# Second MoE: seven-product up products on halves of 256 columns, one plain block of 256 tokens, TensorE's order written out

## The chip, the cores and the metric

The kernel runs on one core of one Trainium2 chip. The metric is the device time of one execution in microseconds (us); three executions of the kernel before have a median of 1143.99 us (1142.7 to 1144.92).

## The reference

Three steps follow one another. An attention with a memory term (4 batches, 8 heads, 576 positions, 64 wide) gives 2304 tokens of 512 values. The first MoE is a gated layer of width 1536, the second a layer of width 2048 with a bounded square:

```python
g = x @ w_gate                      # 2304x512 @ 512x1536
silu = g * (1.0 / (1.0 + np.exp(-g)))
x = silu * (x @ w_val) @ w_out      # first MoE: back to 2304x512
h = x @ w_in                        # second MoE: 2304x512 @ 512x2048
g = np.where(h >= 1, h, np.where(h <= -1, 0.0, (h + 1) ** 2 / 4.0))
out = g @ w_out                     # 2304x512
```

Weights arrive as float64 words. Each product is made to about fp32 exactness out of two fp32r parts (hi and lo) of both operands, so that one tile product costs three matmuls: hi by lo, lo by hi, hi by hi (`PARTS`).

## The kernel before, in words

A program of tasks (`Plan`) is built in Python. Each task has an engine, a cost, a priority, the tasks it depends on and the buffer places that it uses. `Plan.order` simulates the engines with these costs and emits the instructions in the order of the simulation, so every engine's order is fixed at build time; at run time the engines wait for each other by semaphores. All large DMAs are issued by SyncE (SP) in the same order, and an SP instruction that waits holds up those behind it.

**Attention** (up to about 345 us) also makes gate and value products of the first six width units for tokens 0 to 1535 and stores them to DRAM (`early_unit`, `gv`). **The first MoE** then runs over six blocks of 384 tokens (`BLOCK`): first the remaining early products (all eight early units for the two late blocks, units 6 and 7 for the others), then block by block twelve width units. `hidden` makes one: either it loads gate and value from `gv`, or TensorE makes them (`up_matmuls`, moving operand 384 columns); ScalarE and VectorE form the product and split it into hi and lo (`ends_of`); `down` adds its share into four PSUM banks (moving operand `h`, 384 columns). At the end of a block `pieces` copies the four banks out and stores seven pieces of the block (`ys`).

**The second MoE** uses a seven-product scheme (Winograd's form of Strassen's). For a pair of width units and a block the up product is a 2x2 by 2x2 product of blocks: 256 by 128 blocks of weights, and halves of the block of tokens (`HB`, 192 columns). Seven block products of six matmuls each (42 in all) take the place of eight (48). Sums of weight blocks are made when a pair is decoded (`Weights.pair`: three places of 512 KB and one of 256 KB), sums of tokens in `pieces`. `hidden2` (L1343) issues the products: t1 and t5 into two banks, t6, t2, t7, t4 accumulate into them. In between ScalarE copies a bank (`seed`, `keep`) before TensorE goes on accumulating in it, and VectorE adds two results (v1, v2); t4 waits for v2. Each of the two results goes through relu, square, bound, hi and lo, and `down` (L1416) multiplies it by the second weights: per width unit nine matmuls of 512 columns for the three 128-token groups of a block.

The 16 width units form eight pairs, in three phases of 2, 3 and 3 pairs (`PHASES`). Each phase goes over all six blocks, loads the block's seven pieces (`load_y`), and adds into partial sums that are kept in DRAM between phases (`part`). In which order TensorE takes the products and the `down` groups is left to the priorities of the plan.

The weights of the second MoE are decoded from float64 by VectorE and ScalarE in the background. Of the first three pairs (`PARK`) the decoded places are stored to DRAM while the first MoE runs, and fetched back before their use (`parked`, `back`); the other five are decoded into place during the second MoE. SBUF has 25 unit places (`UNITS`), six half places (`HALVES`), 15 places for token pieces (`XB`).

Of the kernel before, what the change touches and what calls it, by code (L numbers as in the profile page):

```python
# [18 lines left out]
P = 128  # L19
# [21 lines left out]
XB, OP, RAW, HP, TP, WA = 15, 5, 3, 3, 3, 5  # L41
SU = 2
UNITS, HALVES = 25, 6
PHASES = (2, 3, 3)
PARK = 3
# [4 lines left out]
BLOCK = 384  # L50
# [210 lines left out]
def e_pe(n, cols):  # L261

    return n * (cols + (32 if cols >= 320 else 18)) / 2.4
# [879 lines left out]
def tile_attention_two_moe(  # L1143
# [14 lines left out]
    NB = NT // BLOCK  # L1158
    ys = [[dram.tile([P, 4 * HB], F32, name=f"ys{b}_{k}") for k in range(7)] for b in range(NB)]
    part = [[dram.tile([P, DM], F32, name=f"part{b}_{m}") for m in range(BLOCK // P)] for b in range(NB)]  # L1160
# [96 lines left out]
    plan.cap("W", UNITS, range(UNITS1))  # L1257
    for tag, n in (("wh", HALVES), ("xb", XB), ("hp", HP), ("tp", TP), ("op", OP), ("su", SU), ("mm", 4), ("acc", 4),
                   ("gv", 3), ("dd", 1)):
        plan.cap(tag, n)  # L1260
# [6 lines left out]
    blocks = [slice(e, e + BLOCK) for e in range(0, NT, BLOCK)]  # L1267
# [15 lines left out]
    def ends_of(s, t, src, uses):  # L1283


        def hi():
            s["h"] = hp.tile([P, 2, BLOCK], F32R, name="h", tag=f"h{s['i'].slot}")
            nc.scalar.copy(s["h"][:, 0], s["t"])  # L1288

        def lo():  # L1290
            nc.vector.tensor_sub(s["h"][:, 1], s["t"], f32(s["h"][:, 0]))  # L1291

        t = plan.add("ACT", e_act(BLOCK), s["at"], hi, [t], [s["it"], s["i"]])
        s["done"] = plan.add("DVE", e_dve2(BLOCK), s["at"], lo, [t], [s["it"], s["i"]])
        return s

    def start_of(base):
        return {"i": plan.inst("hp"), "it": plan.inst("tp"), "at": base}

    def mk_t(s):  # L1300
        s["t"] = tp.tile([P, BLOCK], F32, name="t", tag=f"t{s['it'].slot}")
        return s["t"]

    def hidden(f, tok, base, x, kind):


        s = start_of(base)
        if kind == 0:
            i_g, i_v = plan.inst("xb"), plan.inst("gv")

            def load():
                s["gv"] = xb.tile([P, 2, BLOCK], F32, name="gv", tag=f"xb{i_g.slot}")
                nc.sync.dma_start(s["gv"], gv[f][:, :, tok])

            src = [(lambda j=j: s["gv"][:, j], i_g) for j in range(2)]
            t_g = plan.dma(base - 25, [BLOCK * 2.85], load, uses=[i_g, i_v], behind=xlast.get(plan))
            xlast[plan] = plan.last
        else:
# [3 lines left out]
            def prod():  # L1322
                for j, u in enumerate(units):
                    s[j] = mm.tile([P, HT], F32, name="mm", tag=f"mm{banks[j].slot}")
                    up_matmuls(nc, s[j][:, 0:BLOCK], u, x["x"], slice(0, BLOCK))

            t_g = plan.add("PE", e_pe(len(units) * 12, BLOCK), base + 1, prod,
# [3 lines left out]
            src = [(lambda j=j: s[j][:, 0:BLOCK], i_p) for j, i_p in enumerate(banks)]  # L1331
# [7 lines left out]
        t = plan.add("ACT", e_act(BLOCK) + 60, base, silu, [t_g] + (downs[-2:-1] if kind else downs[-3:-2]), [src[0][1], s["it"]])  # L1339
        t = plan.add("DVE", e_dve2(BLOCK), base, product, [t, t_g], [src[1][1], s["it"]] + ([i_v] if kind == 0 else []))  # L1340
        return ends_of(s, t, src, [])

    def hidden2(pair, y, base, up):  # L1343


        banks = i_a, i_e = [plan.inst("mm") for _ in range(2)]
        i_d, i_k, i_s, i_u = plan.inst("acc"), plan.inst("dd"), plan.inst("su"), plan.inst("su")
        s = {}
        two = [start_of(base), start_of(base)]
        lf, rt = slice(0, HB), slice(HB, BLOCK)  # L1350

        def product(k, out, first):
            for j in range(2):
                for i, (pw, px) in enumerate(PARTS):
                    nc.tensor.matmul(out, pair["k"](k, pw, j), y["x"][k][:, px, j], start=first and not (i or j),  # L1355
                                     stop=(j == 1 and i == 2), skip_group_check=True)

        def some(*todo):
            for k, name, first in todo:
                if name not in s:  # L1360
                    i = i_d if name == "d" else (i_a, i_e)[name == "e"]
                    s[name] = (acc if name == "d" else mm).tile(
                        [P, HT], F32, name=("acc" if name == "d" else "mm"), tag=f"{i.tag}{i.slot}")
                product(k, s[name][:, lf], first)

        def pe(prio, todo, deps, uses, **kw):
            ks = [k for k, *_ in todo]
            return plan.add("PE", e_pe(6 * len(todo), HB), prio, lambda: some(*todo),
                            deps + [y["t"][k] for k in ks], uses + pair["i"] + [y["i"][k] for k in ks], **kw)

        def keep(name, src):
            def f():
                i = i_s if name == "s5" else i_u
                s[name] = su.tile([P, HB], F32, name=name, tag=f"su{i.slot}")
                nc.scalar.copy(s[name], s[src][:, lf])  # L1375
            return f

        def seed():
            s["e"] = mm.tile([P, HT], F32, name="mm", tag=f"mm{i_e.slot}")
            nc.scalar.copy(s["e"][:, lf], s["a"][:, lf])  # L1380

        cost = e_act(HB)
        t1 = pe(up + 1, [(0, "a", True)], pair["t"], [i_a, i_e], behind=(ups or [None])[-1])
        ups.append(t1)
        t5 = pe(up, [(4, "d", True)], [t1], [i_d, i_k])
        c1 = plan.add("ACT", cost, base - 10, seed, [t1], [i_a, i_e])
        c5 = plan.add("ACT", cost, base - 10, keep("s5", "d"), [t5], [i_d, i_s])
        t6 = pe(up - 10, [(5, "a", False)], [t5, c1], [i_a])
        c2 = plan.add("ACT", cost, base - 10, keep("u2", "a"), [t6], [i_a, i_u])
        t2 = pe(up - 10, [(1, "e", False), (2, "d", False)], [t6, c5], [i_e, i_d])  # L1390
        t7 = pe(up - 10, [(6, "a", False)], [t2, c2], [i_a])
        v1 = plan.add("DVE", e_dve2(HB), base - 10,
                      lambda: nc.vector.tensor_add(s["e"][:, rt], s["u2"], s["d"][:, lf]), [c2, t2], [i_e, i_d, i_k, i_u])  # L1393
        v2 = plan.add("DVE", e_dve2(HB), base - 10,
                      lambda: nc.vector.tensor_add(s["a"][:, rt], s["s5"], s["a"][:, lf]), [t7, c5], [i_a, i_s])
        t4 = pe(up - 10, [(3, "a", False)], [v2], [i_a])
        for h, (name, i_p, t) in enumerate((("e", i_e, v1), ("a", i_a, t4))):
            o = two[h]
            src = lambda name=name: s[name][:, 0:BLOCK]

            def relu(o=o, src=src):
                nc.scalar.activation(mk_t(o), src(), AF.Relu, bias=half, scale=0.5)  # L1402

            def square(o=o):
                nc.scalar.activation(o["t"], o["t"], AF.Square)  # L1405

            def bound(o=o, src=src):
                nc.vector.scalar_tensor_tensor(o["t"], src(), 1.0, o["t"], op0=ALU.max, op1=ALU.min)  # L1408

            t = plan.add("ACT", e_act(BLOCK), base, relu, [t], [i_p, o["it"]])  # L1410
            t = plan.add("ACT", e_act(BLOCK), base, square, [t], [o["it"]])
            t = plan.add("DVE", e_dve2(BLOCK), base, bound, [t], [i_p, o["it"]])
            ends_of(o, t, None, [])
        return two
# [22 lines left out]
    def pieces(state, b, base, t_d, later):  # L1437
# [5 lines left out]
        places = [plan.inst("xb") for _ in range(7)]  # L1443
        st = {}
        lf, rt = slice(0, HB), slice(HB, BLOCK)
# [8 lines left out]
        def copies(eng, m0, left, right):  # L1454
            def f():
                for cols, k in ((lf, left), (rt, right)):
                    for j in range(2):
                        eng(raw(k)[:, j], state[m0 + j][:, cols])
            return f

        ca = plan.add("ACT", 4 * e_act(HB), base, copies(nc.scalar.copy, 0, 0, 6), [t_d],
                      [*state["i"][:2], places[0], places[6]])
        cb = plan.add("DVE", 4 * e_dve2(HB), base, copies(nc.vector.tensor_copy, 2, 1, 2), [t_d],
                      [*state["i"][2:], places[1], places[2]])
        sub = nc.vector.tensor_sub
        d1 = plan.add("DVE", e_dve2(BLOCK), later, lambda: sub(raw(4), raw(6), raw(0)), [ca],
                      [places[0], places[4], places[6]])
        d2 = plan.add("DVE", e_dve2(BLOCK), later, lambda: sub(raw(5), raw(2), raw(4)), [cb, d1],
                      [places[2], places[4], places[5]])
        d3 = plan.add("DVE", e_dve2(BLOCK), later, lambda: sub(raw(6), raw(2), raw(6)), [d1, cb],  # L1470
                      [places[2], places[6]])
        d4 = plan.add("DVE", e_dve2(BLOCK), later, lambda: sub(raw(3), raw(1), raw(5)), [d2],
# [134 lines left out]
```

## Time and profile before

| | |
|---|---|
| median of three executions | 1143.99 us |
| profiled execution, its own time | 1142.59 us |
| span of that execution on the core | 1140.8 us |
| TensorE matmul busy | 1109.7 us, 97% |
| TensorE weight load busy (beside the matmuls) | 1013.6 us, 89% |
| VectorE, ScalarE, GpSimd busy | 769.1, 677.5, 257.8 us |
| granted TensorE clock, mean over the span | 0.994 of full speed |

Matmuls are pipelined, so a record lasts longer than the distance to the next one. What a matmul costs TensorE in a stream is the distance from start to start: the start of the next row less the start of this one, over the count. The three stages stand in the trace at 0 to 345.5 us (attention), 345.5 to 703 us (first MoE) and 703 us to the end (second MoE).

### The profile page before, as it was taken

The page shows a single profiled execution, that of the slowest core. Times are in us where ns is not written, and L with a number is a line of the kernel's source. Part 1 is how long each engine was busy: PE and PEld are TensorE (multiplying, and loading weights), DVE is VectorE, ACT ScalarE, POOL GpSimd, SP SyncE. Part 2 cuts the span into 40 slices and gives each one's busy share as a digit, 9 for nine tenths or more (in the row PEclk, how much of TensorE's full clock was granted, in tenths as well). Part 3 has the DMA queues.
Part 4 walks back from the last instruction along what each step waited for, and adds up shares of the span by engine and source line. Part 5 has one row for each costly group of instructions (what it writes and reads, how often), then busy time and mean ns, then how long its engine had stood idle before and what let it go on. Part 6 is the DMA issues. An engine that isn't in the chain of part 4 may idle for free.

```text
span 1140.8 us, 20230 instructions
## 1 busy us (share of the span) xinstructions
PE 1109.7 (97%) x6864; PEld 1013.6 (89%) x6864; DVE 769.1 (67%) x1863; ACT 677.5 (59%) x1650; POOL 257.8 (23%) x325
## 2 busy tenths in 40 slices
PE   6998999999999999999999999999999999999998
PEld 4566887898889999999999999899999999999997
DVE  5689979988872888888962553876677335734334
ACT  6888989999882355454542433755655444544443
POOL 6898779666560000000000000000000000000000
PEclk9999999999999999999999999999999999999999
DMA  5566556756538889769796639986755456545412
GB/s 137 161 181 173 138 148 165 198 145 162 168 98 301 294 278 384 226 245 354 271 338 202 238 132 383 389 294 216 254 194 185 162 180 219 175 157 183 150 57 83
DMA packets 181816, 240.04 MB, mean 210 GB/s; under 512 B 73936, under 2 KB 127184, under 8 KB 181712
## 3 DMA queue, kind: packets, MB, share of 16 engines
q1 hardware_dynamic: 181136, 237.69, 63.9%
q8 instruction: 55, 0.90, 0.3%
q10 hardware_dynamic: 576, 1.05, 0.2%
q14 instruction: 49, 0.40, 0.1%
HBM read 163.98 MB, written 67.63 MB: 203 GB/s over the span
## 4 chain that ended last, share of the span: by engine, by line
PE 78%; ACT 8%; DMA 6%; DVE 2%; issue 2%; POOL 1%; SPq 0%; POOLq 0%; ACTq 0%; DVEq 0%
PE acc L1426 30%; PE mm L1138 20%; PE mm L1355 14%; PE acc L1355 6%; PE av L868 3%; DMA KK<-KK 2%; ACT a L682 2%; PE s L669 1%; DMA raw<-in_moe_w_gate_dram 1%; DMA raw<-in_moe_w_out_dram 1%; ACT R L398 1%; PE t L807 1%; DMA gv<-gvo 1%; ACT KK L398 1%; PE s L703 1%
## 5 line engine op out<-in xcount | busy, mean ns | idle before, releaser
L1426 PE MATMUL acc<-wu,h 128*128 128x512 f32 x864 | 215.0, 394 | 1.6 <-DVE h L1291 1.6
L1138 PE MATMUL mm<-xb,wu 128*128 128x384 f32 x1152 | 204.2, 334 | 0.9 <-ACT gvo L1186 0.9
L1138 PEld LDWEIGHTS mm<-xb,wu 128*128 128x128 f32 x1152 | 200.1, 188 | 1.3 <-ACT gvo L1186 1.2
L1426 PEld LDWEIGHTS acc<-wu,h 128*128 128x128 f32 x864 | 156.0, 189 | 31.5 <-DVE h L1291 2.2
L1288 ACT CAST h<-t 128x384 fp32r<-128x384 f32 x168 | 85.7, 513 | 130.4 <-PE acc L1426 69.9
L1426 PE MATMUL acc<-h,wu 128*128 128x384 f32 x864 | 154.2, 334 | 0.3 <-DVE h L1291 0.3
L1426 PEld LDWEIGHTS acc<-h,wu 128*128 128x128 f32 x864 | 150.0, 188 | 0.7 <-DVE h L1291 0.7
L1355 PE MATMUL mm<-xb,wu 128*128 128x192 f32 x1152 | 149.0, 273 | 0.0
L1355 PEld LDWEIGHTS mm<-xb,wu 128*128 128x128 f32 x1152 | 143.8, 191 | 4.8
L1291 DVE TENSOR_TENSOR h<-t,h 128x384 fp32r<-128x384 f32 x168 | 92.2, 556 | 68.2 <-ACT h L1288 67.7
L1138 PE MATMUL mm<-xh,wu 128*128 128x512 f32 x432 | 115.7, 406 | 0.9 <-DMA xh<-xs 0.6
L1402 ACT ACTIVATE t<-mm,half 128x384 f32<-128x384 f32 x96 | 55.2, 581 | 93.3 <-DVE mm L1393 51.1
L760 POOL TENSOR_SCALAR a<-a,r,OGP 128x256 f32<-128x256 f32 (+3 forms) x144 | 96.1, 677 | 29.3 <-DVE r L751 10.9
L1408 DVE SCALAR_TENSOR_TENSOR t<-mm,t 128x384 f32<-128x384 f32 x96 | 52.9, 555 | 65.0 <-ACT t L1405 64.9
L1138 PEld LDWEIGHTS mm<-xh,wu 128*128 128x128 f32 x432 | 78.0, 191 | 16.0 <-DMA xh<-xs 1.5
L1355 PE MATMUL acc<-xb,wu 128*128 128x192 f32 x576 | 79.9, 274 | 0.3 <-ACT s L1375 0.2
L682 ACT ACTIVATE a<-a,mn 128x128 f32<-128x128 f32 (+3 forms) x128 | 71.1, 559 | 10.5 <-DVE mn L675 10.0
L1355 PEld LDWEIGHTS acc<-xb,wu 128*128 128x128 f32 x576 | 72.5, 192 | 1.2 <-ACT s L1375 0.4
L955 ACT ACTIVATE wA<-raw 128x512 f32<-128x512 f32 x64 | 43.1, 673 | 46.4 <-DMA raw<-in_moe_w_out_dram 23.1
L1186 ACT COPY gvo<-mm 128x384 f32<-128x384 f32 (+1 forms) x84 | 43.4, 524 | 36.6 <-PE mm L1138 23.0
L1393 DVE TENSOR_TENSOR mm<-u,acc 128x192 f32<-128x192 f32 x48 | 17.3, 361 | 68.4 <-PE acc L1355 68.1
L675 DVE CUSTOM_DVE_ANT_0 a<-s,mask 128x256 f32<-128x256 f32 (+3 forms) x128 | 57.7, 484 | 5.9 <-PE s L669 3.6
(158 smaller groups left out, 1842.1 us busy)
## 6 DMA issues: line engine op xcount, KB each, us to landing
xb<-ys SPq DMA_DIRECT2D x126, 384.0 KB, 4.2
xb<-xs SPq DMA_DIRECT2D x48, 384.0 KB, 6.4
gv<-gv SPq DMA_DIRECT2D x48, 384.0 KB, 5.1
ys<-yo SPq DMA_DIRECT2D x42, 384.0 KB, 3.9
raw<-in_moe_w_out_dram SPq DMA_DIRECT2D x28, 512.0 KB, 4.7
xs<-x SPq DMA_DIRECT2D x16, 576.0 KB, 3.3
gv<-gvo SPq DMA_DIRECT2D x48, 192.0 KB, 4.4
part<-oo SPq DMA_DIRECT2D x36, 256.0 KB, 2.2
```

Of the source, the lines that this page charges most:

```text
L675: nc.vector.tensor_tensor_reduce(a, st[f"s{h}{c}"][:, 0:kl], self.mask0[:, 512 - kl:512], -0.125, 3.0e38, ALU.add, ALU.min, mn[:, o:o + 1])
L682: nc.scalar.activation(a, a, AF.Exp, bias=mn[:, o:o + 1], scale=-1.0, accum_out=sm[:, o, 0:1])
L760: nc.gpsimd.tensor_scalar(a, a, st["mn"]["r"][:, o:o + 1], self.OGP[:, n, o:o + 1], op0=ALU.mult, op1=ALU.mult)
L955: nc.scalar.activation(f32(s["F"]), f32(words(s["raw"])[:, :, 1]), AF.Abs)
L1138: nc.tensor.matmul(out, kt_of(unit, pw, kt), x[kt][:, px, cols], start=(kt == 0 and i == 0), stop=(kt == KT - 1 and i == 2))
L1186: nc.scalar.copy(s["o", j], s[j][:, 0:gt])
L1288: nc.scalar.copy(s["h"][:, 0], s["t"])
L1291: nc.vector.tensor_sub(s["h"][:, 1], s["t"], f32(s["h"][:, 0]))
L1355: nc.tensor.matmul(out, pair["k"](k, pw, j), y["x"][k][:, px, j], start=first and not (i or j), stop=(j == 1 and i == 2), skip_group_check ...
L1402: nc.scalar.activation(mk_t(o), src(), AF.Relu, bias=half, scale=0.5)
L1408: nc.vector.scalar_tensor_tensor(o["t"], src(), 1.0, o["t"], op0=ALU.max, op1=ALU.min)
L1426: nc.tensor.matmul(state[m][:, 0:n], l, r, start=(begin and i == 0), stop=(end and i == 2), skip_group_check=True)
```

## The change

- `BLOCKS` replaces the six equal blocks: four of 512 tokens and one of 256 (tokens 1536 to 1791), which is the second in order. Both stages use it. `HB` becomes 256.
- In the second MoE the blocks of 512 keep the seven-product form, now with 256 columns (`hidden2`). The block of 256 tokens takes the plain eight products (`hidden1`), which read three stored pieces instead of seven.
- TensorE's instructions of the second MoE are one chain (`next_pe`, each behind the last). `down2` does half of a `down` (two 128-token groups, six matmuls); the halves of the pair before stand in `queue`, and `fill` puts one after t5, one before t4 and the rest after t4. The third bank of `hidden2` comes from the pool `mm`, since a block of 512 tokens takes all four banks of `acc`.
- In phases 1 and 2 the plain block comes last (`ORDERS`). The last block of the first MoE takes the units that need products first (`LAST`).
- All eight pairs are parked. They are decoded into three unit places and one half place of their own (tags `B`, `Bh`), and `fetch_pair` brings them back: for the coming phase from the third block of a phase on.
- Places: `XB` 15 to 12 (each a third larger), `UNITS` 25 to 20, `HALVES` 6 to 5.

The diff, cut to its core:

```diff
-XB, OP, RAW, HP, TP, WA = 15, 5, 3, 3, 3, 5
+XB, OP, RAW, HP, TP, WA = 12, 5, 3, 3, 3, 5
-UNITS, HALVES = 25, 6
+UNITS, HALVES = 20, 5
-PARK = 3
-BLOCK = 384
+BLOCK = 512
+BLOCKS = ((0, 512), (1536, 256), (512, 512), (1024, 512), (1792, 512))
+LAST = (8, 9, 10, 11, 0, 1, 2, 3, 4, 5, 6, 7)
+ORDERS = ((0, 1, 2, 3, 4), (0, 2, 3, 4, 1), (0, 2, 3, 4, 1))
 HB = BLOCK // 2
...
-    return n * (cols + (32 if cols >= 320 else 18)) / 2.4
+    return n * (cols + (32 if cols >= 320 else 25)) / 2.4
...
+    plan.cap("B", 3 + UNITS, range(UNITS))
+    plan.cap("Bh", 1 + HALVES, range(HALVES))
...
+    def next_pe(cost, prio, fn, deps, uses):
+        seq.append(plan.add("PE", cost, prio, fn, deps, uses, behind=seq[-1:]))
+        return seq[-1]
+
+    def fill(n):
+        for go in queue[:n]:
+            go()
+        del queue[:n]
+
+    def hidden1(pair, y, base, ahead):
+        two = []
+        for todo in (((0, 0), (1, 1)), ((4, 0), (3, 2))):
+            i_p, s = plan.inst("mm"), start_of(base, HB)
...
+            t = next_pe(e_pe(12, HB), base, prod, pair["t"] + [y["t"][piece] for _, piece in todo],
+                        [i_p] + pair["i"] + [y["i"][piece] for _, piece in todo])
+            if not ahead:
+                fill((len(queue) + 1) // 2 if not two else len(queue))
+            two.append(bounded(s, t, i_p, lambda s=s: s["p"][:, 0:HB]))
+        return two
...
+        t1 = pe([(0, "a", True)], pair["t"], [i_a, i_n])
+        t5 = pe([(4, "d", True)], [], [i_d, i_k])
+        c1 = add_act(lambda: nc.scalar.copy(bank("e")[:, lf], s["a"][:, lf]), [t5], [i_a, i_e])
+        c5 = add_act(keep("s5", "d", i_s), [t5], [i_d, i_s])
+        fill(1)
+        t6 = pe([(5, "a", False)], [c1], [i_a])
+        c2 = add_act(keep("u2", "a", i_u), [t6], [i_a, i_u])
+        t2 = pe([(1, "e", False), (2, "d", False)], [c5], [i_e, i_d])
+        t7 = pe([(6, "a", False)], [c2], [i_a])
+        v1 = add_dve("e", "u2", "d", [c2, t2], [i_e, i_d, i_k, i_u])
+        v2 = add_dve("a", "s5", "a", [t7, c5], [i_a, i_s])
+        fill(1)
+        t4 = pe([(3, "a", False)], [v2], [i_a, i_n])
+        fill(len(queue))
...
-            pairs[p] = wts.pair(plan, "W", "wh", [in_cols(moe2_w_in, f) for f in (2 * p, 2 * p + 1)], pr, behind, p < PARK)
+            pairs[p] = wts.pair(plan, "B", "Bh", [in_cols(moe2_w_in, f) for f in (2 * p, 2 * p + 1)], pr, behind, True)
...
+    def fetch_pair(ph, i, after):
+        p, pr = first_of[ph] + i, at_(ph, 0) + 20 * i - 15
+        for s in (pairs[p], w_out[2 * p], w_out[2 * p + 1]):
+            wts.back(plan, s, ("W", "W", "W", "wh"), pr, fetched + after)
+            fetched[:] = [s["load"]]
...
     for ph, count in enumerate(PHASES):
+        last = ph == len(PHASES) - 1
+        for k, b in enumerate(ORDERS[ph]):
+            tok, at0 = blocks[b], at_(ph, k)
+            y = load_y(b, at0, [t_last] if ph == 0 else [], y["last"], free=0) if ph or k else y0
+            if not last and 1 < k:
+                fetch_pair(ph + 1, k - 2, [y["last"]])
...
+                hid = hidden2 if size(tok) == BLOCK else hidden1
+                for j, s in enumerate(hid(pairs[p], y, pb, last and k == len(blocks) - 1 and i == count - 1)):
+                    for ms in ((0, 1), (2, 3))[:state["n"] // 2]:
+                        queue.append(lambda s=s, state=state, ms=ms, base=pb, p=p, f=2 * i + j, b=b, at0=at0, count=count,
+                                     last=last: down2(s, state, ms, base + 25, w_out[2 * p + f % 2], f == 0,
+                                                      f == 2 * count - 1, last, b, at0))
+    fill(len(queue))
```

## Rows read from the trace of the kernel before

**Rows 1.** The page: busy time, share of the span and instructions by engine.

```profile
PE 1109.7 (97%) x6864; PEld 1013.6 (89%) x6864; DVE 769.1 (67%) x1863; ACT 677.5 (59%) x1650; POOL 257.8 (23%) x325
```

**Rows 2.** Busy time by stage: from:to, us, engines (instructions), clock, DMA share, GB/s.

```profile
345.50:703.20 357.70, 356.46 (x2038) 353.44 (x2037) 239.62 (x497) 153.27 (x324) 1.43 (x1) 1.00 0.80 277
703.20:1140.80 437.60, 431.76 (x2917) 394.14 (x2916) 246.73 (x516) 224.28 (x506) 0.00 (x0) 1.00 0.58 198
```

**Rows 3.** TensorE's waits from 345 us on: who for whom, us, times, longest.

```profile
PE acc L1426 <- DVE h L1291: 2.0, 3, 0.9
PE mm L1138 <- ACT gvo L1186: 0.9, 1, 0.9
PE acc L1355 <- ACT s L1375: 0.2, 1, 0.2
```

**Rows 4.** Timeline of TensorE in the second MoE: start, length, instruction, tiles, shape, count.

```profile
905.66 0.81 PE L1355 MATMUL mm<-xb,wu 128*128 128x192 f32 x6
906.31 0.83 PE L1355 MATMUL acc<-xb,wu 128*128 128x192 f32 x6
906.98 2.24 PE L1426 MATMUL acc<-wu,h 128*128 128x512 f32 x9
909.05 1.48 PE L1355 MATMUL mm<-xb,wu 128*128 128x192 f32 x12
...
911.74 0.64 PE L1426 MATMUL acc<-wu,h 128*128 128x512 f32 x2
```

**Rows 5.** Timeline of TensorE's weight loads in the same stretch.

```profile
910.98 0.75 PEld L1355 LDWEIGHTS acc<-xb,wu 128*128 128x128 f32 x6
911.65 0.19 PEld L1426 LDWEIGHTS acc<-wu,h 128*128 128x128 f32 x1
```

**Rows 6.** Timeline of TensorE in the attention, two matmuls of 256 columns, then 128.

```profile
261.76 0.28 PE L669 MATMUL s<-KK,SX 128*128 128x256 f32 x1
...
262.00 0.33 PE L669 MATMUL s<-KK,SX 128*128 128x128 f32 x2
```

**Rows 7.** The chain of waits in the first MoE, a stretch of 384-column matmuls.

```profile
474.55 4.16 PE acc L1426 x24
```

**Rows 8.** Timeline of TensorE, a stream of 512 columns and the next start.

```profile
345.51 12.79 PE L1138 MATMUL mm<-xh,wu 128*128 128x512 f32 x54
358.13 0.34 PE L1138 MATMUL mm<-xb,wu 128*128 128x384 f32 x1
```

**Rows 9.** Timeline of TensorE at the seam of the two MoEs.

```profile
703.18 0.81 PE L1355 MATMUL mm<-xb,wu 128*128 128x192 f32 x6
703.83 6.43 PE L1426 MATMUL acc<-h,wu 128*128 128x384 f32 x36
...
719.42 2.34 PE L1426 MATMUL acc<-wu,h 128*128 128x512 f32 x9 [0.78 <-DVE h L1291]
```

**Rows 10.** Groups of ScalarE and VectorE in the second MoE: busy, mean ns, idle before.

```profile
L1402 ACT ACTIVATE t<-mm,half 128x384 f32<-128x384 f32 x96 | 55.2, 581 | 93.3 <-DVE mm L1393 51.1 <-PE mm L1355 42.1
...
L1375 ACT COPY u<-mm 128x192 f32<-128x192 f32 x48 | 15.3, 319 | 21.9 <-PE mm L1355 18.2 <-DVE mm L1395 1.9 <-DVE h L1291 0.7
...
L1018 DVE TENSOR_TENSOR wu<-wA,wu 128x512 fp32r<-128x512 f32 x15 | 10.3, 687 | 2.1 <-ACT wu L1016 2.1
```

**Rows 11.** SP's queue: the first raw weights of the second MoE, and all parks.

```profile
467.18 0.99 SPq L950 DMA_DIRECT2D raw<-in_moe_w_in_dram  x2
...
L1023 SPq DMA_DIRECT2D park<-wu x15: 319/332/923, 481.6 to 578.0; - x15
```

**Rows 12.** DMA issues: piece loads (count, KB, us to landing), and the longest in the chain.

```profile
xb<-ys SPq DMA_DIRECT2D x126, 384.0 KB, 4.2
...
808.37 10.20 DMA raw<-in_moe_w_out_dram
```

**Rows 13.** Timeline at the end of the kernel.

```profile
1134.60 2.34 PE L1426 MATMUL acc<-wu,h 128*128 128x512 f32 x9 [0.87 <-DVE h L1291]
1135.60 2.07 DVE L1564 TENSOR_TENSOR oo<-oo,acc 128x512 f32<-128x512 f32 x3 [1.05 <-PE acc L1426]
```

## What I predict, and why

> **What bounds the kernel now.** I read the page first: TensorE's matmuls are busy 97% of the span [rows 1]. A busy share of pipelined matmuls says little by itself, so I read next what TensorE waits for. From 345 us to the end it waits for other engines 3.1 us in all [rows 3], in some 790 us: both MoEs are bound by TensorE's own stream. Last I read what a matmul costs there, from start to start in the timelines:
> - 192 columns: 12 in 906.98 - 905.66 = 1.32 us, then 24 in 911.74 - 909.05 = 2.69 us [rows 4]; together 36 in 4.01 us, **111.4 ns** each.
> - 384 columns: 24 in 4.16 us [rows 7], **173.3 ns**.
> - 512 columns: 9 in 909.05 - 906.98 = 2.07 us [rows 4], **230 ns**; in a long stream 54 in 358.13 - 345.51 = 12.62 us [rows 8], **233.7 ns**.
> - 256 columns: two in 262.00 - 261.76 = 0.24 us [rows 6], so about **118 to 120 ns**. Such pairs stand only in the attention.
>
> From 384 to 512 columns the price per column holds (0.451 and 0.449 to 0.456 ns), and 256 columns fit (0.46 to 0.47). At 192 it is 0.58: the line through 256 and 384 would give some 91 ns, and 20 ns are lost. The weight loads show where: in a 192-column run one starts every (911.65 - 910.98)/6 = 112 ns [rows 5], the matmuls' own pace. A matmul of 192 columns is over before the next 128x128 weights are in; one of 256 columns lasts longer than the load.
>
> The model closes. The second MoE has 6 blocks x 8 pairs x 42 = 2016 matmuls of 192 columns (224.6 us) and 6 x 3 x 16 x 3 = 864 of 512 (199.6 us at 231). With 36 matmuls of the first MoE that run in its stretch [rows 9] (6.2 us) that is 430.4 us; from 703.18 us [rows 9] to the last matmul's end, 1134.60 + 2.34 = 1136.94 us [rows 13], it is 433.8. Of the 3.4 us left, 0.8 and 0.9 are two waits [rows 9, 13].
>
> **The change, part by part**, against the profiled execution (1142.59 us), which is 1.4 us under the median of the three runs.
>
> *Up products of the second MoE.* Four blocks of 512 need 4 x 8 x 42 = 1344 matmuls of 256 columns, the plain block 8 x 2 units x 4 x 3 = 192: 1536 in all. At 118.5 ns that is 182.0 us instead of 224.6: **-42.6 us**. Columns hardly change (393216 for 387072); 480 matmuls at the weight load's pace go. The row [rows 6] stands between other shapes, so both ends: not under the loads' pace, 111.4 ns (171.1 us, -53.5), and not likely over 124 ns, the line's price with 5 ns of jitter (190.5 us, -34.1). The `down` matmuls stay at 864 of 512 columns.
>
> The Trainium skill (TensorE: Matmul & The Clock Gate, "LDWEIGHTS (loading the stationary operand)") gives a weight load its columns over 1.2 GHz, 107 ns for 128; the loads' 112 ns [rows 5] lie 5 ns above that and bear the rule out. The same page ("Back-to-back issue gap") puts an isolated matmul at N/2.4 + 2.5 ns, 109 ns for 256 columns, under this trace's 118 to 120; by it, as an estimate, the up products would take some 168 us. The measured pair decides here.
>
> *First MoE.* 6 x 12 x 12 = 864 `down` matmuls of 384 columns become 576 of 512 and 144 of 256; 1152 products become 720 of 512 and 288 of 256. Before: 2016 x 173.4 = 349.6 us. After: 1296 of 512 at 231.5 (between 230 and 233.7) and 432 of 256 at 118.5: 300.0 + 51.2 = 351.2 us, **+1.6** (-4 if 512 columns cost 227, +5 at 234). 288 matmuls fewer bring nothing, because 512 columns cost as much per column as 384.
>
> *Start of the first MoE.* The one wait there, 0.9 us for ScalarE's copies [rows 3], comes from stores of gate and value. Five buffers of 256 columns hold two thirds of what five of 384 did, while 256-column products run first: **+1** (0 to 4).
>
> *Seam of the MoEs.* With 12 piece places, `y0` holds seven and five are left for the seven pieces of the last block, so VectorE's sums must wait until two have been stored; the next block's pieces wait for these sums. The first pair has no older `down` to put between its products, so t6 waits for ScalarE's copy and t4 for VectorE's sum. Before, the seam cost 0.78 us at 719 us [rows 9] and little else. **+3** (0 to 10).
>
> *TensorE's written order.* Each pair of 512 tokens has four guarded steps. t1 or t5 is 6 x 118.5 = 0.71 us, half a `down` 6 x 231 = 1.39 us. Behind t5, t6 waits for c1, with 1.39 us of `down` as cover; a 192-column copy takes 0.32 us [rows 10], so one of 256 some 0.4 us. t7 waits for c2 under t2 (1.42 us), t4 for v2 under the second half `down` (1.39 us). All fit with over 0.5 us to spare, as long as ScalarE and VectorE are free; an operation of 0.6 to 0.7 us in front [rows 10] eats that. What is queued behind such a wait is all of TensorE. The chain to the first `down` of a result is relu, square, bound, hi, lo: five steps of 0.6 to 0.7 us (0.58 us at 384 columns, 0.69 us on VectorE at 512 [rows 10]) and the handovers, about 4.8 us, against 6.9 us of TensorE's work between. The copies' wait before was 0.2 us in all 48 pairs [rows 3]. For 40 pairs **+2** (0 to 8).
>
> *Weights.* Five more pairs are stored and fetched: some 28 MB more traffic (twice five pairs of 5 x 512 + 256 KB), with no new work on the compute engines. Three pairs passed the decoder from 467 to 578 us [rows 11], 37 us each; eight at that pace end at 467 + 296 = 763 us. The last is needed in phase 2, from about 703 + 96 + 144 = 943 us on. TensorE hides it with 180 us to spare, and the DMA queues, at 0.80 and 0.58 of their time in the two stages [rows 2], have room. Nothing on the path; were the pace 60 us a pair, it would start to show.
>
> *Tail.* The last block has two 128-token groups instead of three: one VectorE sum of 2.07/3 = 0.69 us less [rows 13]; and the last pair's own `down` stands behind 2.8 us of older `down`, which covers the wait of 0.87 us [rows 13]. **-1.5.**
>
> Sum: -42.6 + 1.6 + 1 + 3 + 2 - 1.5 = -36.5. 1142.59 - 36.5 = 1106.1, with 1.4 for the median **1107.5 us**.
>
> **Rivals.**
> 1. *256 columns run at the weight load's pace.* If only the load limits, 111.4 ns instead of 118.5: 10.9 us less, **1097 us**. Against it: the pair in rows 6, and that 256 lies on the line of the larger sizes. To this side the Trainium skill's isolated gap leads (TensorE: Matmul & The Clock Gate, "Back-to-back issue gap"). 0.13.
> 2. *The seam and the written order cost more.* One strict chain gives up what the plan did before, to take whatever is ready. 0.5 us lost in each of 40 pairs, or one late pieces' load per block visit of some 1.5 us: 15 to 20 us, **1125 us**. For it: ScalarE and VectorE still decode weights in the first phases. Against it: the covers above. 0.17.
> 3. *Slower: pieces arrive late at every block visit.* The place is `load_y` on SP's queue. Of 12 places the running block holds seven, so the next block's last two pieces are asked for only when t1 and t5 of the running block's last pair are done. From there to t7 of the next block are 9.1 + 4.9 = 14 us. A piece took 4.2 us at 384 KB [rows 12], some 5.6 at 512 KB; the longest load on the chain took 10.2 us [rows 12]. Eleven visits would each have to lose 3.7 us to eat the gain, that is loads of 18 us: **1148 us**. SP would have to be held up behind a fetch or a store for that. 0.05.
> 4. *DMA of parked weights holds back the first MoE as well*, a milder form: **1135 us**. 0.03.
>
> **How the numbers follow.** My forecast, 1101 to 1113 us, has 0.62; the rivals have 0.13, 0.17, 0.05 and 0.03. The range takes rival 1 to about 1096 (256 columns at 111) and rival 2 to 1124: 1096 to 1124 holds some 0.8. A measurement of this kernel can tell about 0.2% (2.3 us) from no change; all cases but rival 3 lie far below: faster 0.94, same 0.01, slower 0.05.
>
> **What would show it.** Right: in the second MoE six 256-column matmuls start to start in 0.71 us, weight loads no longer at their own pace; 512 columns at 230 ns in the first MoE; TensorE's waits from 345 us on under 12 us; the second MoE some 390 us long. Wrong: a pitch of 112 or over 124 ns; waits on ScalarE's copies or on `h` that recur per pair; waits on piece loads at the block visits; first MoE products beyond 234 ns; VectorE still decoding after 800 us with TensorE waiting for weights.

## The result and the profile after

The changed kernel takes **1113.85 us** (median of four, 1111.40 to 1115.46) against 1143.35 us beside it: a ratio of 0.9739, 95% interval 0.9714 to 0.9764, so 2.6% faster. The forecast was 1107.5 us with a range of 1096 to 1124. The sign and the main term came out as forecast. The time lies 6 us above the forecast: waits, and what the clock took behind them, cost more than was booked.

The page's engine line of the changed kernel; its span is 1113.4 us:

```profile
PE 1069.7 (96%) x6096; PEld 921.0 (83%) x6096; DVE 767.4 (69%) x1754; ACT 656.8 (59%) x1506; POOL 256.8 (23%) x325
```

Against [rows 1], TensorE has 768 instructions fewer, and the weight loads' share falls from 89% to 83%. The timeline of TensorE in the second MoE, changed kernel (start, length, instruction, shape, count), answers to [rows 4]:

```profile
860.73 3.04 PE L1373 MATMUL mm<-xb,wu 128*128 128x256 f32 x24
863.61 1.55 PE L1625 MATMUL acc<-wu,h 128*128 128x512 f32 x6
864.99 0.88 PE L1373 MATMUL mm<-xb,wh 128*128 128x256 f32 x6
865.71 2.91 PE L1625 MATMUL acc<-wu,h 128*128 128x512 f32 x12
868.45 1.60 PE L1373 MATMUL mm<-xb,wu 128*128 128x256 f32 x12
```

24 matmuls of 256 columns take 863.61 - 860.73 = 2.88 us, 120.0 ns each, above the 112 ns of a weight load [rows 5], so that the loads no longer set the pace. The written order is there too: t6, t2 and t7 (24 matmuls), half a `down`, t4, two halves, t1 and t5. The chain of waits in the first MoE, answering to [rows 7]:

```profile
612.64 5.44 PE mm L1140 x24
```

24 matmuls of 512 columns in 5.44 us, 226.7 ns each. By stage (from:to, us, engines, clock, DMA share, GB/s), answering to [rows 2], and the 120 us around and behind the seam:

```profile
345.50:699.50 354.00, 346.33 (x1711) 295.73 (x1711) 251.14 (x482) 151.46 (x285) 1.44 (x1) 0.99 0.79 279
699.50:1113.40 413.90, 403.23 (x2473) 361.99 (x2471) 228.46 (x423) 205.25 (x401) 0.00 (x0) 0.99 0.74 277
700.00:820.00 120.00, 114.33 (x676) 101.55 (x675) 71.47 (x134) 64.23 (x126) 0.00 (x0) 0.97 0.99 381
```

The second MoE's DMA share has risen from 0.58 to 0.74, and from 700 to 820 us the queues are full (0.99). TensorE's waits from 345 us on (who for whom, us, times, longest), answering to [rows 3]:

```profile
PE mm L1140 <- ACT gvo L1188: 5.2, 1, 5.2
PE acc L1625 <- DVE h L1298: 4.0, 3, 2.0
PE mm L1373 <- DVE mm L1439: 3.0, 2, 2.2
PE acc L1469 <- DVE h L1298: 2.4, 1, 2.4
```

They have grown from 3.1 to 14.6 us. And behind each long wait stands something that my sum did not have. Windows of the changed kernel before, just behind and after the wait of 5.2 us, then behind two more (the clock is the figure before the last two):

```profile
364.00:370.00 6.00, 6.00 (x53) 6.00 (x52) 4.78 (x11) 0.68 (x2) 0.00 (x0) 1.00 1.08 380
375.60:381.10 5.50, 5.50 (x25) 5.50 (x26) 3.76 (x9) 1.97 (x5) 0.00 (x0) 0.50 0.50 186
381.20:387.00 5.80, 5.80 (x49) 5.80 (x49) 5.80 (x14) 2.17 (x5) 0.00 (x0) 0.99 0.52 163
725.60:729.30 3.70, 3.70 (x13) 3.16 (x14) 3.45 (x6) 2.12 (x5) 0.00 (x0) 0.56 0.90 296
800.90:804.20 3.30, 3.30 (x11) 2.60 (x10) 2.66 (x6) 2.20 (x4) 0.00 (x0) 0.53 0.91 356
```

TensorE looks fully busy from 375.6 to 381.1 us, but it starts 25 matmuls where 49 to 53 fit into stretches of like length: the granted clock is 0.50, the lower of its two levels (1.2 instead of 2.4 GHz). Behind the wait of 2.4 us it is the same, by the count: 24 matmuls in 4.63 us, where 24 x 0.12 us and the last one's end make 3.0; the granted clock is 0.62 from 548.1 to 552.6 us.

```profile
548.15 4.63 PE L1469 MATMUL acc<-h,wu 128*128 128x256 f32 x24 [2.43 <-DVE h L1298]
```

### The profile page after: what moved, and what is told of

The parts are those of the page before. It is cut to its first block, busy times and chain, and to the rows that moved or that the text cites. A ratio compares the mean times of both kernels' runs of the same rounds, so it can differ in the third digit from the quotient of the medians.

```text
span 1113.4 us, 18370 instructions
## 1 busy us (share of the span) xinstructions
PE 1069.7 (96%) x6096; PEld 921.0 (83%) x6096; DVE 767.4 (69%) x1754; ACT 656.8 (59%) x1506; POOL 256.8 (23%) x325
## 4 chain that ended last, share of the span: by engine, by line
PE 80%; ACT 7%; DMA 5%; DVE 3%; issue 1%; POOL 1%; SPq 0%; ACTq 0%; DVEq 0%; POOLq 0%
PE mm L1140 23%; PE acc L1625 18%; PE mm L1373 16%; PE acc L1469 13%; PE av L870 4%; PE s L671 2%; DMA gv<-gvo 1%; ACT a L684 1%; DMA KK<-KK 1%; PE t L809 1%; PE s L705 1%; ACT KK L400 1%; ACT R L400 1%; DMA gv<-gv 1%; PE s L667 1%
## 5 line engine op out<-in xcount | busy, mean ns | idle before, releaser
L1140 PE MATMUL mm<-xb,wu 128*128 128x512 f32 (+1 forms) x1008 | 203.8, 362 | 5.2 <-ACT gvo L1188 5.2
L1373 PE MATMUL mm<-xb,wu 128*128 128x256 f32 x1296 | 168.6, 283 | 0.0
L1469 PE MATMUL acc<-h,wu 128*128 128x512 f32 (+1 forms) x720 | 153.2, 371 | 2.4 <-DVE h L1298 2.4
L1298 DVE TENSOR_TENSOR h<-t,h 128x512 fp32r<-128x512 f32 (+1 forms) x140 | 88.3, 635 | 57.7 <-ACT h L1295 57.0
L1295 ACT CAST h<-t 128x512 fp32r<-128x512 f32 (+1 forms) x140 | 80.3, 576 | 80.6 <-PE acc L1469 31.4
L1357 ACT ACTIVATE t<-mm,half 128x512 f32<-128x512 f32 (+1 forms) x80 | 51.8, 648 | 93.7 <-PE mm L1373 47.2
L684 ACT ACTIVATE a<-a,mn 128x128 f32<-128x128 f32 (+3 forms) x128 | 71.1, 558 | 12.5 <-DVE mn L677 12.1
L1188 ACT COPY gvo<-mm 128x512 f32<-128x512 f32 (+1 forms) x80 | 43.2, 545 | 57.4 <-PE mm L1140 41.0
L1363 DVE SCALAR_TENSOR_TENSOR t<-mm,t 128x512 f32<-128x512 f32 (+1 forms) x80 | 50.7, 634 | 32.1 <-ACT t L1360 32.1
L1439 DVE TENSOR_TENSOR mm<-u,mm 128x256 f32<-128x256 f32 x32 | 13.7, 429 | 85.6 <-PE mm L1373 81.5
L404 DVE TENSOR_TENSOR R<-t,R 128x384 fp32r<-128x384 f32 (+3 forms) x120 | 53.3, 483 | 4.5 <-ACT R L400 3.8
L968 DVE SCALAR_TENSOR_TENSOR wA<-raw,wA 128x512 uint32<-128x512 uint32 x68 | 55.2, 815 | 0.4
```

The lines of the kernel that those rows point to most:

```text
L404: nc.vector.tensor_sub(lo(), src(), f32(hi()))
L684: nc.scalar.activation(a, a, AF.Exp, bias=mn[:, o:o + 1], scale=-1.0, accum_out=sm[:, o, 0:1])
L968: nc.vector.scalar_tensor_tensor(s["F"], words(s["raw"])[:, :, 1], 0xC0000000, s["F"], op0=ALU.bitwise_and, op1=ALU.bitwise_or)
L1140: nc.tensor.matmul(out, kt_of(unit, pw, kt), x[kt][:, px, cols], start=(kt == 0 and i == 0), stop=(kt == KT - 1 and i == 2))
L1373: nc.tensor.matmul(out, pair["k"](k, pw, j), y["x"][piece][:, px, j], start=first and not (i or j), stop=last and j == 1 and i == 2, skip_ ...
L1469: nc.tensor.matmul(state[m][:, 0:n], l, r, start=(begin and i == 0), stop=(end and i == 2), skip_group_check=True)
```

## The experiments

**Is it the weight load that sets the pace at 192 columns?** My theory rests on that, so I took columns away from the kernel before, where it says that nothing would be gained:

```diff
-                    nc.tensor.matmul(out, pair["k"](k, pw, j), y["x"][k][:, px, j], start=first and not (i or j),
+                    n = HB if first and not (i or j) else 128
+                    nc.tensor.matmul(out[:, 0:n], pair["k"](k, pw, j), y["x"][k][:, px, j, 0:n], start=first and not (i or j),
```

> The kernel before, with 40 of the 42 matmuls of each up product of the second MoE on 128 of their 192 columns; a third of the columns of these products is left out. Theory (the weight load sets the pace at 192 columns): start to start stays at 109 to 112 ns, the second MoE stays 430 to 436 us long, the time 1138 to 1146 us. Rival (a matmul costs its columns plus 13 ns, 67 ns for 128): 1920 x 44 ns = 85 us less, about 1060 us.

Measured: 1138.28 us (one execution), beside 1141.8 for the kernel before. A third of the columns of the up products is gone, and the time stays within 0.3%. Timeline of TensorE in that kernel:

```profile
906.11 0.84 PE L1356 MATMUL mm<-xb,wh 128*128 128x128 f32 x6
906.78 0.83 PE L1356 MATMUL acc<-xb,wu 128*128 128x192 f32 x6
907.45 2.27 PE L1427 MATMUL acc<-wu,h 128*128 128x512 f32 x9
```

Six matmuls take 0.67 us from start to start in both rows, in the first all with 128 columns, in the second five of six: 112 ns, as with 192 in [rows 4]. The rival, a price of the columns plus 13 ns (67 ns), is out. That the floor is the weight load, and not another fixed cost of the same size, rests on the loads' own rows, which start every 112 ns [rows 5]; no run here changed the load. The 112 ns agree with the Trainium skill (TensorE: Matmul & The Clock Gate, "LDWEIGHTS (loading the stationary operand)"), whose rule gives 107 ns for 128 weight columns. With 256 columns the measured 120.0 ns is past that floor and follows the columns at 2.4 GHz: 106.7 + 13.3 ns. The same 13.3 ns stand in 384 columns (173.3 = 160.0 + 13.3, [rows 7]) and in 512 in the first MoE (226.7 = 213.3 + 13.4). The gap of N/2.4 + 2.5 ns that the Trainium skill gives for an isolated matmul (TensorE: Matmul & The Clock Gate, "Back-to-back issue gap") would be, as an estimate, 109 ns; in this stream of loads and matmuls the measurement decides against it.

**Width or order?** The changed kernel back on six blocks of 384, with its order and its parking:

```diff
-BLOCK = 512
-BLOCKS = ((0, 512), (1536, 256), (512, 512), (1024, 512), (1792, 512))
+BLOCK = 384
+BLOCKS = tuple((e, 384) for e in range(0, NT, 384))
-ORDERS = ((0, 1, 2, 3, 4), (0, 2, 3, 4, 1), (0, 2, 3, 4, 1))
+ORDERS = (tuple(range(6)),) * 3
-            if not last and 1 < k:
+            if not last and 1 < k < 5:
-                    for ms in ((0, 1), (2, 3))[:state["n"] // 2]:
+                    for ms in ((0, 1), (2,)):
```

> The changed kernel with six blocks of 384 tokens again, halves of 192 columns; TensorE's written order, the parking of all pairs and the numbers of places stay. Theory (the width of the halves is the gain): 2016 x 111.4 instead of 1536 x 120 ns is +40 us, 2016 x 173.4 instead of 1296 x 227 and 432 x 120 ns in the first MoE +4 us, less some of the waits of the changed kernel that come with its block of 256 (some 10 us): 1140 to 1156 us. Rival (the written order is the gain): 1110 to 1122 us.

Measured: 1162.94 us, ratio 1.0201 (1.0172 to 1.0229): 49 us slower than the changed kernel and 2% slower than the kernel before. Timeline of TensorE in it:

```profile
1003.46 0.81 PE L1373 MATMUL mm<-xb,wh 128*128 128x192 f32 x6
1004.11 2.26 PE L1625 MATMUL acc<-wu,h 128*128 128x512 f32 x9
1006.20 1.48 PE L1373 MATMUL mm<-xb,wu 128*128 128x192 f32 x12
1007.75 1.64 PE L1625 MATMUL acc<-wu,h 128*128 128x512 f32 x6
```

Six matmuls of 192 columns take 1004.11 - 1003.46 = 0.65 us, the old pace; the 12 in the last but one row take 1007.75 - 1006.20 = 1.55 us up to the next instead of 1.34, a wait of 0.2 us that comes back in the next block. So the width is more than the whole gain: at the old width the rest of the change costs some 20 us. It came out 7 us above my range: I had taken much of its waits to go with the block of 256, but they sum to 13.7 us, hardly less than the changed kernel's 14.6. With equal waits the sum is 1114 + 40 + 4 = 1158 us; the other 5 us were not taken apart.

**Is the written interleave worth anything?** The up products keep their order, the `down` halves are placed by the plan:

```diff
-        t = next_pe(e_pe(3 * len(ms), DM), base, prod, [s["done"], unit["t"]],
-                    [s["i"], unit["i"]] + [state["i"][m] for m in ms])
+        mine = state.setdefault(ms, [])
+        t = plan.add("PE", e_pe(3 * len(ms), DM), base, prod, [s["done"], unit["t"]],
+                     [s["i"], unit["i"]] + [state["i"][m] for m in ms], behind=mine[:None if end else 1])
+        mine.append(t)
```

> The changed kernel with the down halves of the second MoE out of TensorE's chain: the plan places them by priority, only the up products stay in their written order. Theory (TensorE has work enough beside the copies in either order): 1108 to 1120 us, waits from 345 us on within 8 us of the changed kernel. Rival (the written interleave is what covers the copies and sums): each of 40 pairs loses 0.5 to 1 us, 1132 to 1154 us.

Measured: 1120.85 us (0.9827, 0.981 to 0.9844), 7 us slower than the changed kernel (10 us by the two ratios to the kernel before) and 1 us beyond my theory's end. TensorE's waits in the second MoE of that kernel:

```profile
PE mm L1373 <- DVE mm L1439: 7.3, 12, 1.0
PE acc L1625 <- DVE h L1298: 4.6, 8, 0.6
PE mm L1373 <- ACT mm L1444: 3.2, 4, 1.0
```

15.1 us in 24 places of up to 1.0 us, where the changed kernel has 7.0 us in five. So the interleave hides copies and sums, worth 7 to 10 us: less than my rival's 0.5 us per pair, more than nothing. The extra waits are 8 us; against them this profile lost less at the lower clock (mean granted 0.997, in the changed kernel 0.990).

**The wait of 5.2 us at the start of the first MoE.** Timeline of the changed kernel: a run of 256-column products, ScalarE's copies, the run after the wait.

```profile
357.98 12.39 PE L1140 MATMUL mm<-xb,wu 128*128 128x256 f32 x102
...
375.18 1.02 ACT L1188 COPY gvo<-mm 128x256 f32<-128x256 f32 x3 [8.71 <-DMA gv<-gvo]
...
375.61 7.66 PE L1140 MATMUL mm<-xb,wu 128*128 128x256 f32 x41 [5.23 <-ACT gvo L1188]
```

ScalarE is idle for 8.7 us because all five store buffers are under way; the queues are full (share 1.08, 364 to 370 us above). The chain of waits has the first store of this block:

```profile
364.84 10.24 DMA gv<-gvo
```

Its copy was done at 360.7 us. SP issued it 4.1 us later, behind four token loads (360.13 to 364.53 us) and the landing of an earlier store (364.78 us), and it took 10.24 us to land. Five buffers of 256 columns are filled in 5 x 12 x 0.12 = 7.2 us, five of 512 in 5 x 12 x 0.227 = 13.6 us. So the 512-token late block goes first:

```diff
-    for h, tok in enumerate(late + [g for g in blocks if g not in late]):
+    for h, tok in enumerate(late[::-1] + [g for g in blocks if g not in late]):
```

> The changed kernel with the two late blocks of the early products in the other order: 512 tokens first, then 256. Theory (five store buffers of 256 columns are full after 7 us, before the first store has landed): the wait of 5.2 us at 370 us shrinks to 0 to 1.5 us, and the 2.5 us that the matmuls behind it lose at half clock go with it: 1104 to 1109 us. Rival (the stores land late behind the loads whichever block is first): a wait of over 4 us stays, 1111 to 1116 us.

Measured: 1102.91 us (0.9659, 0.9638 to 0.968), 11 us faster than the changed kernel. The timeline of TensorE there runs through:

```profile
358.32 26.01 PE L1140 MATMUL mm<-xb,wu 128*128 128x512 f32 x114
```

Wait and half clock are gone, 7.6 us together; the wait for `h` at 548 us fell from 2.4 to 0.4 us as well, which I had not expected and which, with 1.6 us at half clock behind it, makes up the rest. In that stretch of the changed kernel ScalarE had waited 2.1 and 1.0 us for loads of gate and value, and it still waits 0.4 and 1.7 us for them in this one. That the small block wants twice as many loads per time fits, but why less of it reaches TensorE here was not tested.

**The waits for VectorE's sum.** All further runs start from that kernel. Timeline of VectorE in the changed kernel while TensorE waits 2.2 us (797.5 to 800.1 us):

```profile
797.45 0.42 DVE L965 TENSOR_SCALAR wA<-wA 128x512 uint32<-128x512 uint32 x1
797.78 0.68 DVE L1363 SCALAR_TENSOR_TENSOR t<-mm,t 128x512 f32<-128x512 f32 x1
798.38 0.68 DVE L987 TENSOR_TENSOR wA<-wA,wS 128x512 f32<-128x512 f32 x1
798.98 0.68 DVE L968 SCALAR_TENSOR_TENSOR wA<-raw,wA 128x512 uint32<-128x512 uint32 x1
799.58 0.42 DVE L1439 TENSOR_TENSOR mm<-s,mm 128x256 f32<-128x256 f32 x1
```

v2 (L1439) stands last, behind two decoding steps and the other result's bound. Without the decoding of three pairs:

```diff
+            if p >= 5:
+                o, w = pairs[p - 5], {}
+                pairs[p] = dict(o, i=list(o["i"]), w=w, k=lambda k, part, j, w=w, at=o["at"]: w[at[k][0]][
+                    :, part, at[k][1] + j * P:at[k][1] + (j + 1) * P])
+                for f in (2 * p, 2 * p + 1):
+                    w_out[f] = dict(w_out[f - 10])
+                continue
```

> The changed kernel with the 512-token late block first (1102.9 us), in which the last three of the eight weight pairs of the second MoE aren't decoded: their places are fetched from what pairs 0 to 2 left in DRAM, so a part of the second MoE is computed with the wrong weights, and three pairs' decoding and stores (some 57 us of VectorE, 9 MB of loads and 9 MB of stores) are left out. Theory (decoding on VectorE in the first phase stands in front of the sums that TensorE waits for): the waits at 709 to 715 us and 786 us with their half clock (some 10 us) fall to under 4 us: 1094 to 1099 us. Rival (the waits belong to the written order at the seam, with no older down to put between): at most 2 us less, 1101 to 1105 us.

Measured: 1100.7 us (0.9641, 0.9602 to 0.9679). TensorE's waits from 345 us on:

```profile
PE acc L1632 <- DVE h L1298: 4.3, 3, 2.0
PE mm L1373 <- DVE mm L1439: 0.8, 1, 0.8
PE acc L1469 <- DVE h L1298: 0.3, 1, 0.3
```

Both were half right. The wait of 2.2 us for the sum, which the kernel that it starts from has as well, is gone, so that one goes with the decoding (or with its loads and stores, which this kernel leaves out too; VectorE's rows above speak for the decoding). The waits at the seam (0.8 and 2.0 us) stay, so they do not. In time nothing can be told: the kernel that it starts from took 1102.91 us and, in a later run, 1100.53.

**The seam.** The first pair's products are ranked ahead of the last `down`s of the first MoE:

```diff
-                pb = at0 + 20 * i
+                pb = at0 + 20 * i if ph or k or i else 580
```

> The kernel with the 512-token late block first, with the products of the very first pair of the second MoE ranked ahead of the last downs of the first MoE, so that these stand between its steps. Theory (the seam waits because nothing older is left to put between): the waits of 1.0 and 2.2 us at 709 and 712 us and their half clock go, 3 to 5 us less: 1098 to 1101 us. Rival (VectorE, busy with decoding and pieces, is late whatever stands between): 1102 to 1106 us.

Measured: 1100.91 us (0.9648, 0.9607 to 0.9689). A second run of both kernels on one chip:

> The kernel with the 512-token late block first, once more beside the next one on the same chip: 1101 to 1105 us.

> The kernel that also ranks the first pair's products ahead of the last downs of the first MoE, beside the one before on the same chip. Theory (the seam's 3 us come back as waits for piece loads): within 3 us of it. Rival (the seam's gain stays): 3 to 5 us less.

Measured: 1100.53 us (0.9641, 0.9626 to 0.9657) and 1101.07 us (0.9638, 0.9623 to 0.9654). Timeline of TensorE at the seam, first without, then with the new rank:

```profile
708.07 0.97 PE L1373 MATMUL mm<-xb,wh 128*128 128x256 f32 x6 [0.81 <-DVE mm L1439]
708.88 1.59 PE L1373 MATMUL mm<-xb,wu 128*128 128x256 f32 x12
712.51 1.62 PE L1625 MATMUL acc<-wu,h 128*128 128x512 f32 x6 [2.03 <-DVE h L1298]
```

```profile
707.32 0.88 PE L1373 MATMUL mm<-xb,wh 128*128 128x256 f32 x6
708.04 2.91 PE L1469 MATMUL acc<-h,wu 128*128 128x512 f32 x12
710.78 1.59 PE L1373 MATMUL mm<-xb,wu 128*128 128x256 f32 x12
712.22 1.55 PE L1625 MATMUL acc<-wu,h 128*128 128x512 f32 x6
```

With an older `down` between the steps both waits go, which settles their cause. The time doesn't follow. With the new rank TensorE waits 2.4 us for pieces (`xb<-ys`) at 758 us in the first run, 2.1 us for ScalarE at 760 us in the second. All waits from 345 us on still fall from 7.6 to 5.7 us in the second runs, but the mean granted clock falls from 0.995 to 0.992. So within the crowded stretch behind the seam one wait gives way to another; why the clock takes the rest was not tested. These two kernels are the fastest that I have, and can't be told apart.

**The plan's price of a 256-column matmul**, 117 ns, set to the measured 120:

```diff
-    return n * (cols + (32 if cols >= 320 else 25)) / 2.4
+    return n * (cols + 32) / 2.4
```

> The kernel with the 512-token late block first, with the plan's price of a 256-column matmul set to the measured 120 ns (256 + 32 instead of 256 + 25 cycles). Nothing is computed otherwise; the order of ScalarE, VectorE and SP can change. Theory (VectorE's order was simulated with a TensorE that is a few per cent too fast or too slow): the waits for sums behind decoding (2.4 us at 786 us, with its half clock) shrink, 1098 to 1102 us. Rival (the order of the other engines is set by loads and free places, not by this price): 1102 to 1105 us.

Measured: 1102.73 us (0.9663, 0.9629 to 0.9697), with the same five waits in the second MoE (7.0 us). The price made no difference that can be told.

**Places.** The decoder's pace was not what I had reckoned. SP's timeline of the changed kernel, the first and the last of the eight pairs' loads:

```profile
454.26 1.10 SPq L952 DMA_DIRECT2D raw<-in_moe_w_in_dram  x2
...
913.13 1.53 SPq L952 DMA_DIRECT2D raw<-in_moe_w_in_dram  x2
```

(913.13 - 454.26)/7 = 66 us a pair, not 37. Two kernels take a piece place away; one of them gives it to the decoder as a fourth place:

```diff
-XB, OP, RAW, HP, TP, WA = 12, 5, 3, 3, 3, 5
+XB, OP, RAW, HP, TP, WA = 11, 5, 3, 3, 3, 5
...
-    plan.cap("B", 3 + UNITS, range(UNITS))
+    plan.cap("B", 4 + UNITS, range(UNITS))
```

> The kernel with the 512-token late block first, with 11 instead of 12 piece places and nothing else changed. Theory (piece loads hide behind 14 us of products): waits for pieces stay under 3 us in all, 1100 to 1106 us. Rival (the places were the limit): each of 11 block visits loses 1 us or more, over 1112 us.

> The kernel with the 512-token late block first, with four instead of three unit places for decoding, paid for with 11 instead of 12 piece places. Theory (the three places set the decoder's pace, some 60 us a pair where the kernel before took 37): pairs pass in 40 to 50 us, the last decoding loads stand before 870 us instead of 913 us. Rival (VectorE is too busy for a faster pace): over 57 us a pair, last loads after 890 us. The time: with one piece place fewer, 1099 to 1106 us.

Measured: 1106.11 us (0.968, 0.9664 to 0.9697) with 11 piece places alone, 1112.26 us (0.9737, 0.9722 to 0.9752) with the fourth decoding place. SP's loads for the last pair, first with three, then with four decoding places:

```profile
880.43 0.45 SPq L952 DMA_DIRECT2D raw<-in_moe_w_in_dram  x1
```

```profile
791.40 1.62 SPq L952 DMA_DIRECT2D raw<-in_moe_w_in_dram  x2
```

The second pair's stand at 506.4 and 496.7 us, so six pairs take 62 us each with three places and 49 with four. The three places did set the pace. But the kernel with the faster decoder is 6 us slower, and above the range that I gave. TensorE's waits in the second MoE of the kernel with four decoding places are

```profile
PE acc L1625 <- DVE h L1298: 4.9, 3, 2.6
PE mm L1373 <- DMA xb<-ys: 4.3, 6, 1.4
PE mm L1373 <- ACT wA L957: 2.3, 1, 2.3
```

and 1.0 us more. From 345 us on that is 12.5 us, against 11.0 with three decoding places, and the mean granted clock is 0.989 against 0.993; the cause of the difference was not tested. With 11 piece places alone the waits for pieces are 5.3 us in four places, where 12 places in the same order showed none: neither the theory's 3 us nor the rival's 1 us at each visit. Its time, 1106.11 against 1100.53 us with 12 places on the same chip, lies at the theory's end. In this order the cover of 14 us is enough at 12 places and no longer at 11; with the new rank at the seam 12 places had waits for pieces too (3.0 and 0.3 us in the two runs).

## Why the prediction was right, and where it missed

In us, against the profiled executions (spans 1140.8 and 1113.4, a difference of -27.4):

| step of the sum | forecast | measured | from |
|---|---|---|---|
| up products of the second MoE | -42.6 | -40.3 | 1536 x 120.0 = 184.3 for 224.6 |
| matmuls of the first MoE | +1.6 | -4.0 | 1296 x 226.7 + 432 x 120.0 = 345.6 for 349.6 |
| start of the first MoE | +1 | +6.7 | wait 5.2 for 0.9, and 2.4 at half clock |
| rest of the first MoE | 0 | +4 | wait 2.4, some 1.6 at half clock |
| seam and written order | +5 | +8 | waits 7.0 for 2.2 (with the end's 0.9), 3.2 at half clock |
| tail | -1.5 | -0.2 | 3.7 for 3.9 behind the last matmul |

The measured column sums to -25.8; 1.6 us of small differences are left. The forecast was missed by less than its parts: waits, half clock and tail cost 14 us more than booked and the up products gave 2.3 less, while the matmuls of the first MoE gave back 5.6. Without that last piece of luck the time would have been some 1120 us, still within the range.

Of the signs of being right, the pitch came (0.72 us for six, forecast 0.71), and 512 columns in the first MoE were cheaper than the 230 ns named; TensorE's waits did not stay under 12 us (14.6). Of the signs of being wrong, half of one came: decoding goes on after 800 us, but TensorE does not wait for weights. The second MoE was to be some 390 us long. Its stretch is 413.9 us, of which 72 matmuls of the first MoE between the first pair's steps take 16.3 us; the 397.6 us left compare with 431.4 before (437.6 less 6.2 for 36 such matmuls).

- **Up products: right**, mechanism and size. The 120.0 ns measured lies at the upper end of what [rows 6] gave; I took 118.5. Rival 1 is out.
- **512 columns in the first MoE: mis-sized to the good.** I priced them at 231.5 ns, between a row of the second MoE [rows 4] and a stream at the end of the attention [rows 8], and concluded that 288 matmuls fewer bring nothing. In the first MoE they cost 226.7 ns, the low end that I had named, and with a fixed 13.3 ns in each matmul larger blocks save 288 x 13.3 ns = 3.8 us.
- **Start: the mechanism right, the size wrong.** I named the five smaller buffers and gave them 0 to 4 us. The rows that I had read put the old wait at 0.9 us, but not how long a store took: the first landed only at 375 us. The buffers lasted 7.2 us instead of 10.4, and the wait grew by 4.3 us.
- **Half clock: missing from the sum.** 7 us in four places of the profiled execution. Every price in it was for a TensorE at full clock.
- **Rest of the first MoE: missing.** The plain block there takes 1.4 us per width unit where a 512 block takes 2.7, and ScalarE waited there 3.0 us for loads of gate and value. Rival 4, parked weights in the way of the first MoE, is not excluded at this size: the DMA share is 1.02 from 535 to 548 us, and which transfers held these loads up was not tested.
- **Seam and order: rival 2 in a mild form.** The exposed first pair was right (the new rank shows it): waits of 0.8 and 2.0 us and 1.6 at half clock for 0.8 before are +3.7, where I had booked +3. The part of that term that had VectorE's sums wait for free places was not tested. VectorE's decoding in front of a sum was right (the run without it supports it). Placing the `down` halves by hand gained over leaving them to the plan.
- **Weights: the conclusion right, the step wrong.** TensorE never waited for weights, but the pace was 66 us a pair instead of 37. I took the pace from a kernel that decoded into the common pool of 25 unit places; the changed one has three places of its own, and a fourth brought the pace from 62 to 49 us.
- **Tail: the right direction, too large by a little.** The wait of 0.87 us at the end is gone (counted with the order above), but behind the last matmul 0.2 us went instead of 0.7.
- **Rival 3** did not happen: no wait for pieces in the changed kernel.

## What to carry to other kernels

Here a matmul with new weights has a floor of 112 ns, the pace of its weight load: read the distance from start to start at several widths, and below the width at which it stops following the columns, the same columns cost less in fewer, wider matmuls. Whoever changes the size of a block changes every buffer that is counted in tiles, and the small block meets the buffers first: order the blocks so that it doesn't come where the queues are full. A wait of TensorE of 2 us or more may cost more than its length: look at the granted clock behind it, in more than one execution.

## What I had not expected of the hardware

Behind waits of 5.2, 2.4, 2.0 and 2.2 us TensorE ran at the lower clock level for 3 to 5.5 us (granted 0.50 to 0.62 in those windows), so a wait cost up to 1.8 times its length; behind the shorter waits of this kernel (0.8 us at 721 us, 1.3 us at 971 us) the granted clock stayed at 1.00. But the same wait does not always bring it. The row behind the seam's wait in the changed kernel is

```profile
725.59 2.54 PE L1625 MATMUL acc<-wu,h 128*128 128x512 f32 x6 [2.03 <-DVE h L1298]
```

In the second run of the kernel with the 512-token late block first, six such matmuls behind the same wait of 2.03 us take 1.62 us (row at 712.51 us above), at a granted clock of 1.00; and in the kernel with the `down` halves left to the plan, 24 matmuls behind a wait of 2.08 us at 545.76 us take 3.14 us instead of 4.63. What decides it was not tested, and these few us change from one execution to the next.

And 512 columns cost 233.7 ns in a stream at the end of the attention [rows 8], 226.7 in the first MoE and 228 to 230 in the second; what makes the difference was not tried.
